# Tile 0 of a fused attention and mixture kernel: two up stages ahead of two down stages, a new row layout for the down weights, and earlier transposes of the probabilities

## Chip, cores and metric

One core of one Trainium2 chip. The metric is the device time of one launch in microseconds. Time before: 560.77 us, the median of 3 runs (560.01 to 561.48). The core's span in a profile is about 1.7 us shorter than the time of its run.

## The reference, cut to what matters

```python
# q, k, v: (8, 8, 576, 64); retention: scores * decay mask, no softmax
scores = scale * q @ k.T ; ret = scores * gamma ** (i - j) (i >= j) ; x = ret @ v   # -> (4608, 512)
p = domain_probs / (domain_probs.sum(-1) + 1e-9)                                    # (4608, 4)
for e in range(4):
    h = np.maximum(x @ w1[e], 0.0)          # "up":   512 -> 1024
    out += p[:, e:e+1] * (h @ w2[e])        # "down": 1024 -> 512
```

The 4608 tokens are handled in 9 tiles of 512. A batch has 576 tokens, so each ends with a remainder of 64 rows after four chunks of 128.

## The kernel before

An up stage of a tile is 8 steps (32 matmuls with 512 columns, one result tile `ph` a step), a down stage 4 steps (32 matmuls as well, result `po`). The program gives each engine its instructions in one fixed order. In the views, PE is TensorE (matmuls and transposes), PEld its weight loads, DVE is VectorE, ACT ScalarE, POOL GpSimd and SP SyncE; `wt_...` are weights. The plan `at(g, f)` puts attention work behind step g of a tile. Weights are cast from fp32 to bf16 on the way in, which goes through the POOL queue; q, k and v come through the SP queue.

```python
def load_rem(b, gate=None):                  # the 64-row remainder: raw_kr, raw_qr, raw_vr
    ...
        i = nc.sync.dma_start(out=state[b][n + "r"], in_=src[b, :, SM:S, :].rearrange("h p d -> p h d"))
        if gate is not None and n == "k":
            after(i, gate)                   # not before the DMA "gate" has landed
def load_w1(e, part=None): ...               # w1 of expert 0 in two halves of 512 columns, one tile
def load_w2(e): ...
    return nc.gpsimd.dma_start(out=wt2, in_=moe_w2[e].rearrange("(fc p) d -> p fc d", p=128))
...
next(tile0)                                  # first half of the first up matmuls
a0.O(*UNITS[3])
next(tile0)
w20 = load_w2(0)
late_constants()
for e in range(1, E):
    load_w1(e)
    load_w2(e)
load_rem(0, w20)
...
at(1, mixing_weights)                        # 4 transposes of the probabilities, then DVE
at(3, lambda: a0.cast_rem(nc.gpsimd))        # krb, qrb, vrb on POOL
at(20, a0.Trem)                              # PE transposes of qrb, krb
at(22, a0.Srem, a0.Srem_mask)
at(24, a0.Orem)                              # uses vrb
```

## Time and profile before

| | before |
|---|---|
| median of runs | 560.77 us |
| span of the profiled core | 559.2 us |
| PE busy | 545.6 us (98%) |
| PE stands for w2 of expert 0 | 1.74 us, 26.25 to 27.99 |
| PE stands for xT ahead of tile 1 | 0.78 us, before 86.76 |

The engine line and the clock line of the page of the kernel before (the clock has a digit for each fortieth of the span, 9 is 90% or more of full rate):

```profile
PE 545.6 (98%) x3469; PEld 262.5 (47%) x3530; DVE 165.7 (30%) x283; ACT 217.0 (39%) x371; POOL 109.8 (20%) x182
...
PEclk9999999999999999999999999999999999999999
```

PE is the limit, so time can be won only where PE stands, or does work that it need not do. The list of PE's waits up to 95 us, kernel before (in total, times, longest):

```profile
PE pt L437 <- POOL qm L427: 2.3, 3, 1.0
PE po L543 <- DMA wt_492<-in_moe_w_dram: 1.7, 1, 1.7
...
PE ph L514 <- DVE xT L329: 0.8, 1, 0.8
```

`wt_492` is w2 of expert 0. The timeline of the kernel before around it (start, length, engine, line, operation, then the idle time just before and what ended it):

```profile
17.50 0.61 PE L514 MATMUL ph<-xT,wt_269 128*128 128x256 bf16 x4
...
20.73 0.67 PE L206 MATMUL pp<-identf,probs_raw 36*128 36x36 f32 x4
...
27.96 0.72 SPq L115 DMA_DIRECT2D raw_kr<-in_k_dram  x1
...
27.99 6.86 PE L543 MATMUL po<-wt_492,hT 128*128 128x512 bf16 x31 [1.74 <-DMA wt_492<-in_moe_w_dram]
...
40.99 0.60 POOL L243 CAST qrb<-raw_qr 64x512 bf16<-64x512 f32 x1 [3.38 <-DMA raw_qr<-in_q_dram]
...
43.64 0.29 PE L261 MATMUL ptr<-ident,qrb 64*128 64x64 bf16 x4
```

Three things are to be read here. PE stands 1.74 us for w2. The loads of the remainder are issued at 27.96, the moment w2 of expert 0 has landed: that is the gate. And the remainder's transposes at 43.64 have two microseconds to spare after the cast of qrb at 40.99 to 41.59, so the remainder costs PE no waiting.

### The profile page before, as it was taken

To read this page: it belongs to the slowest core of one execution; us is meant where nothing else is said; L and a number is where in the kernel's file an instruction comes from. 1 tells how busy PE (TensorE), PEld (TensorE's weight loads), DVE (VectorE), ACT (ScalarE), POOL (GpSimd) and SP (SyncE) were. 2 spreads that over 40 slices of the span, in tenths; PEclk is the share of its full clock that TensorE was granted. 3 is DMA by queue.
4 is the path that set the end of the run, shared out by engine and by line. 5 is a ranking of instruction groups with operands and counts; after the bars stand their busy time and mean duration, and the time that the engine had idled before them with its cause. 6 is when DMAs were issued, how large, how long until landed. Compare 5 with 4: busy or idle time off the path is not lost.

```text
span 559.2 us, 8453 instructions
## 1 busy us (share of the span) xinstructions
PE 545.6 (98%) x3469; PEld 262.5 (47%) x3530; DVE 165.7 (30%) x283; ACT 217.0 (39%) x371; POOL 109.8 (20%) x182
## 2 busy tenths in 40 slices
PE   7899999999999999999999999999999999999997
PEld 4544455454445444444445444544444444444443
DVE  5402262253214520462035212542046202220222
ACT  6442344433353235323433334323532353335332
POOL 7611247026001520044002600250010000000000
PEclk9999999999999999999999999999999999999999
DMA  9999999591369025910594058803300100010001
GB/s 232 176 203 200 209 206 231 104 213 15 104 131 180 1 84 89 217 28 38 109 179 92 0 123 157 135 1 98 63 2 1 73 3 0 1 76 0 1 0 75
DMA packets 148277, 53.83 MB, mean 96 GB/s; under 512 B 130668, under 2 KB 142188, under 8 KB 148240
## 3 DMA queue, kind: packets, MB, share of 16 engines
q1 hardware_dynamic: 141296, 44.79, 39.2%
q0 software_dynamic: 6800, 8.39, 8.8%
q8 instruction: 27, 0.44, 0.4%
q10 hardware_dynamic: 144, 0.13, 0.1%
q14 instruction: 10, 0.08, 0.1%
HBM read 45.16 MB, written 9.44 MB: 98 GB/s over the span
## 4 chain that ended last, share of the span: by engine, by line
PE 94%; DMA 3%; POOL 1%; issue 1%; SPq 1%; DVE 0%
PE po L543 44%; PE ph L514 43%; DMA wt_492<-in_moe_w_dram 2%; PE o L351 1%; DMA raw_k<-in_k_dram 1%; PE o L365 1%; SPq L85 1%; POOL km L423 0%; PE sr L336 0%; PE orem L358 0%; PE ptc L297 0%; POOL wt_269 L125 0%; PE kvb L389 0%; PE kva L389 0%; PE oc L322 0%
## 5 line engine op out<-in xcount | busy, mean ns | idle before, releaser
L533 ACT ACTIVATE hT<-ph 128x512 bf16<-128x512 f32 x288 | 171.6, 597 | 274.6 <-PE ph L514 274.6
L543 PEld LDWEIGHTS <-hT 128*128 128x128 bf16 x1160 | 112.5, 98 | 134.6 <-DMA wt_492<-in_moe_w_dram 2.2
L549 DVE SCALAR_TENSOR_TENSOR acc<-po,probs,acc 128x512 f32<-128x512 f32 (+1 forms) x109 | 81.3, 746 | 234.6 <-PE po L543 226.8
L514 PE MATMUL ph<-xT,wt_504 128*128 128x512 bf16 x280 | 66.3, 379 | 0.5
L514 PE MATMUL ph<-xT,wt_269 128*128 128x512 bf16 (+1 forms) x303 | 64.2, 362 | 1.4 <-DVE xT L329 0.8
L543 PE MATMUL po<-wt_492,hT 128*128 128x512 bf16 x286 | 63.4, 379 | 1.8 <-DMA wt_492<-in_moe_w_dram 1.7
L543 PE MATMUL po<-wt_506,hT 128*128 128x512 bf16 x273 | 63.8, 379 | 0.8
L514 PE MATMUL ph<-xT,wt_500 128*128 128x512 bf16 x280 | 64.1, 379 | 0.5
L543 PE MATMUL po<-wt_510,hT 128*128 128x512 bf16 (+1 forms) x287 | 63.4, 373 | 0.5
L514 PE MATMUL ph<-xT,wt_508 128*128 128x512 bf16 x286 | 63.7, 379 | 0.2 <-issue 0.2
L543 PE MATMUL po<-wt_502,hT 128*128 128x512 bf16 x280 | 63.4, 379 | 0.4
L403 POOL CAST sbd<-ksum 64x256 bf16<-64x256 f32 x36 | 14.4, 399 | 221.2 <-DVE ksum L408 197.6
L514 PEld LDWEIGHTS <-wt_269 128*128 128x128 bf16 x312 | 30.0, 98 | 32.1 <-issue 0.9
L514 PEld LDWEIGHTS <-wt_508 128*128 128x128 bf16 x288 | 28.0, 98 | 33.3
L514 PEld LDWEIGHTS <-wt_500 128*128 128x128 bf16 x288 | 27.7, 98 | 33.4
L514 PEld LDWEIGHTS <-wt_504 128*128 128x128 bf16 x288 | 26.9, 98 | 30.3
L547 ACT ACTIVATE acc<-po,probs 128x512 f32<-128x512 f32 x36 | 24.7, 687 | 40.1 <-PE po L543 39.1
L235 POOL TENSOR_TENSOR km<-raw_k,gk 128x512 bf16<-128x512 f32 x28 | 29.2, 1043 | 13.9 <-DMA raw_k<-in_k_dram 9.5
L237 POOL CAST vm<-raw_v 128x512 bf16<-128x512 f32 x28 | 17.3, 616 | 41.8 <-PE o L351 34.9
L237 POOL CAST qm<-raw_q 128x512 bf16<-128x512 f32 x28 | 17.1, 611 | 7.4 <-DMA raw_q<-in_q_dram 7.2
L374 DVE TENSOR_TENSOR xT<-o,gq 128x512 bf16<-128x512 f32 x24 | 15.5, 686 | 7.6 <-PE o L365 7.6
L240 POOL TENSOR_TENSOR krb<-raw_kr,gk 64x512 bf16<-64x512 f32 x8 | 8.3, 1037 | 13.8 <-DMA raw_kr<-in_k_dram 13.2
(231 smaller groups left out, 238.7 us busy)
## 6 DMA issues: line engine op xcount, KB each, us to landing
out_dram<-acc SPq DMA_DIRECT2D x35, 256.0 KB, 2.0
raw_k<-in_k_dram SPq DMA_DIRECT2D x32, 256.0 KB, 5.0
raw_q<-in_q_dram SPq DMA_DIRECT2D x32, 256.0 KB, 5.1
raw_v<-in_v_dram SPq DMA_DIRECT2D x32, 256.0 KB, 5.2
wt_269<-in_moe_w_dram POOLq DMA_DIRECT2D x2, 512.0 KB, 5.6
wt_492<-in_moe_w_dram POOLq DMA_DIRECT2D x1, 1024.0 KB, 11.7
wt_500<-in_moe_w_dram POOLq DMA_DIRECT2D x1, 1024.0 KB, 14.5
wt_502<-in_moe_w_dram POOLq DMA_DIRECT2D x1, 1024.0 KB, 20.4
```

The lines of the kernel that those rows point to most:

```text
L85: nc.sync.dma_start(out=pairs_of(state[b][n, hf])[:, h], in_=src[b, h, 256 * hf:256 * hf + 256, :].rearrange("h (p j) d -> p h (j d)", j=2))
L235: eng.tensor_tensor(o, i, gk[:, c, :].unsqueeze(2).to_broadcast([128, H, D]), op=MULT)
L237: eng.tensor_copy(o, i)
L240: eng.tensor_tensor(self.r["k"], self.t["kr"], gk[:R, NCH, :].unsqueeze(2).to_broadcast([R, H, D]), op=MULT)
L351: nc.tensor.matmul(o[64 * j:64 * j + 64, c * C:(c + 1) * C], lhsT=self.m["v"][:, c, 2 * p + j, :], rhs=self.sT[p][:, j, c, :], start=(c == ...
L374: nc.vector.tensor_tensor(xT[:, p, b * S:b * S + SM], o, gq[:, p, 0:SM], op=MULT)
L403: eng.tensor_copy(sbd[r, n, :, r], src[r])
L514: nc.tensor.matmul(ph[:, ts], lhsT=w1_sb[e][:, dc, fc * 128:(fc + 1) * 128], rhs=xT[:, dc, n0 + ts.start:n0 + ts.stop], start=(dc == 0), s ...
L533: nc.scalar.activation(hT[:, fc, :], ph, Relu)
L543: nc.tensor.matmul(po, lhsT=hT[:, fc, ns * 128:(ns + 1) * 128], rhs=w2_sb[e][:, fc, d:d + w], start=(fc == 0), stop=(fc == NFC - 1))
L547: nc.scalar.activation(a, po, Copy, scale=pe)
L549: nc.vector.scalar_tensor_tensor(a, po, pe, a, op0=MULT, op1=ADD)
```

## The change

Intent: in tile 0 only, do up 0 and up 1 before down 0 and down 1, so that PE has work while w2 of expert 0 is still on its way (w1 of expert 1 is therefore loaded ahead of it, in two halves); load w2 with two neighbouring rows in each partition, so that one run in memory (fp32) is 4 KB long instead of 2 KB (the packet records count bf16 bytes); transpose the probabilities in the first wait for w1; take up tile 1 with two early pieces of 384 columns in place of three of 256.

With rows 2i and 2i+1 of a 256-row block in partition i, the hidden units of a block have to come out of the up stage even ones first, then odd ones. So the up stage reads its weight columns with a step of two.

```diff
-        return nc.gpsimd.dma_start(out=wt2, in_=moe_w2[e].rearrange("(fc p) d -> p fc d", p=128))
+        return nc.gpsimd.dma_start(out=wt2[:, :, :].rearrange("p (fo fi) d -> p fo (fi d)", fi=2),
+                                   in_=moe_w2[e].rearrange("(fo p fi) d -> p fo (fi d)", p=128, fi=2))
 ...
-                nc.tensor.matmul(ph[:, ts], lhsT=w1_sb[e][:, dc, fc * 128:(fc + 1) * 128],
+                w = w1_sb[e][:, dc, (fc // 2) * 256:(fc // 2 + 1) * 256].rearrange("p (f i) -> p f i", i=2)
+                nc.tensor.matmul(ph[:, ts], lhsT=w[:, :, fc % 2],
 ...
+        first = [ups(0), ups(1), downs(0), downs(1)] if nt == 0 else [ups(0), downs(0), ups(1), downs(1)]
 ...
-    tiles = [moe(nt, lead=3 if nt < 2 else 0) for nt in range(n_nt)]
+    tiles = [moe(0, lead=3, pause=True), moe(1, lead=2, cut=3 * NT // 4)] + [moe(nt) for nt in range(2, n_nt)]
 ...
+    transposed_probs()
     next(tile0)
     a0.O(*UNITS[3])
     next(tile0)
+    load_w1(1, 0)
+    load_w1(1, 1)
+    late_constants()
     w20 = load_w2(0)
-    late_constants()
-    for e in range(1, E):
+    load_w2(1)
+    for e in range(2, E):
         load_w1(e)
         load_w2(e)
     load_rem(0, w20)
 ...
-            for c, g in enumerate((40, 42, 44, 46)):
+            for c, g in enumerate((39, 41, 43, 45)):
```

Cut here: the constant `identf` is made earlier on POOL, and the chunk work of batch 1 at the end of tile 0 moves into the plan.

More of the change, by code (lines that the diff above doesn't have):

```diff
@@ L156 @@
     make_identity(nc, ident)
+    identf = const.tile([NTT, NTT], FP32)
+    nc.gpsimd.tensor_copy(identf, ident[:NTT, :NTT])
     tri2 = const.tile([128, 2, 128], BF16)
@@ L163 @@
     tri = const.tile([128, 128], BF16)
-    identf = const.tile([NTT, NTT], FP32)
     trir = const.tile([128, R], BF16)
@@ L176, in late_constants @@
                                 base=0, channel_multiplier=-1, pattern=[[1, 128]])
-        nc.gpsimd.tensor_copy(identf, ident[:NTT, :NTT])
     lgp = const.tile([128, NP], FP32)
@@ L201, with transposed_probs @@
     psm = const.tile([128, NTT], FP32)
-    def mixing_weights():
-        pp = ps_at.tile([128, E, NTT], FP32, tag="at", name="pp")
+    def transposed_probs():
+        pp = ps_mm.tile([128, E, NTT], FP32, tag="mm", name="pp")
         for e in range(E):
@@ L207, in mixing_weights @@
         nc.vector.tensor_copy(probs, pp)
+    def mixing_weights():
         nc.vector.tensor_reduce(psm, probs[:, :, :].rearrange("p e t -> p t e"),
@@ L506, in O, with moe @@
                                         gq[:, 2 * u:2 * u + 2, ts], op=MULT)
-    def moe(nt, lead=0):
+    def moe(nt, lead=0, cut=NT // 2, pause=False):
         n0 = nt * NT
@@ L513, in up, with ups @@
             for dc in range(NDC):
-                nc.tensor.matmul(ph[:, ts], lhsT=w1_sb[e][:, dc, fc * 128:(fc + 1) * 128],
+                w = w1_sb[e][:, dc, (fc // 2) * 256:(fc // 2 + 1) * 256].rearrange("p (f i) -> p f i", i=2)
+                nc.tensor.matmul(ph[:, ts], lhsT=w[:, :, fc % 2],
                                  rhs=xT[:, dc, n0 + ts.start:n0 + ts.stop], start=(dc == 0), stop=(dc == NDC - 1))
         acc = [apool.tile([128, Dm], FP32, tag="acc", name="acc") for _ in range(NSUB)]
-        for e in range(E):
-            hT = hpool.tile([128, NFC, NT], BF16, tag="hT")
-            for fc in range(NFC):
-                if e == 0 and fc < lead:
-                    if fc == 0:
-                        early = [ps_mm.tile([128, NT], FP32, tag="mm", name="ph") for _ in range(lead)]
-                        for x in range(lead):
-                            up(early[x], e, x, slice(0, NT // 2))
-                            if x != 1:
-                                yield
+        hTs = {}
+        def ups(e):
+            hT = hTs[e] = hpool.tile([128, NFC, NT], BF16, tag="hT", name="hT")
+            n = lead if e == 0 else 0
+            early = [ps_mm.tile([128, NT], FP32, tag="mm", name="ph") for _ in range(n)]
+            for x in range(n):
+                up(early[x], e, x, slice(0, cut))
+                if pause and x != 1:
+                    yield
+            for fc in range(NFC):
+                if fc < n:
                     ph = early[fc]
-                    up(ph, e, fc, slice(NT // 2, NT))
+                    up(ph, e, fc, slice(cut, NT))
                 else:
@@ L534, in moe, with downs @@
                 yield
+        def downs(e):
+            hT = hTs[e]
             for ns in range(NSUB):
@@ L553, in moe @@
                 yield
+        first = [ups(0), ups(1), downs(0), downs(1)] if nt == 0 else [ups(0), downs(0), ups(1), downs(1)]
+        for stage in first + [g for e in range(2, E) for g in (ups(e), downs(e))]:
+            yield from stage
     a0 = AttP(0)
     UNITS = [(hf, u) for hf in range(2) for u in range(2)]
-    tiles = [moe(nt, lead=3 if nt < 2 else 0) for nt in range(n_nt)]
+    tiles = [moe(0, lead=3, pause=True), moe(1, lead=2, cut=3 * NT // 4)] + [moe(nt) for nt in range(2, n_nt)]
     tile0 = tiles[0]
@@ L619 @@
             at(25, begin1)
-            for c, g in enumerate((40, 42, 44, 46)):
+            for c, g in enumerate((39, 41, 43, 45)):
                 at(g, lambda c=c: state["a1"].Tc(c))
-                if c < 3:
-                    at(g + 1, lambda c=c: state["a1"].Sc(c))
+                at(g + 1, lambda c=c: state["a1"].Sc(c))
                 if c > 0:
@@ L626 @@
                 at(g + 1, lambda c=c: state["a1"].kv(c))
+            at(47, lambda: state["a1"].Oc(3))
         elif nt + 1 < B:
@@ L654 @@
                 f()
-        if nt == 0:
-            state["a1"].Sc(3)
-            next(tiles[1])
-            next(tiles[1])
-            state["a1"].Oc(3)
 _INS = ['q', 'k', 'v', 'moe_domain_probs', 'moe_w1', 'moe_w2']
```

## The prediction

> **What bounds the kernel now.** TensorE: the page shows PE busy 545.6 of 559.2 us, and the chain of waits is 94% PE. A 128x512 matmul starts about every 0.216 us and hides its 98 ns weight load, so only PE idle time can be won. The list of waits and the timeline show: 1.74 us at 26.25-27.99, before tile 0's first down matmul (its w2 landed at 27.95); 0.75 us at 86.0 before tile 1 (waits for the last xT write); 0.6 us of PE time for the four fp32 transposes of probabilities at 20.7.
>
> **What the change should win.** Up 1 fills the 1.74 us. Its two halves should land near 24 and 28, needed at about 26 and 29.3; w2 of expert 0 lands where w1 of expert 1 did (32.97), needed at about 32.9. The transposes' new wait holds only some 0.3 us of slack: gain about 0.3. Tile 1 with two early columns of 384: 0.75 + 0.2. Sum about 3 us. Weight loads with a step of two elements should cost nothing: the Trainium skill ("SBUF — State Buffer", on cachelines) lets bf16 stride up to 8 elements free; this trace doesn't test it.
>
> **What it adds.** The loads of batch 0's 64-row remainder (raw_kr, raw_qr, raw_vr) are gated by w2 of expert 0. Before: gate 27.95, first packets at 31.9 (4 us behind the weight packets already queued), landings 36.57, 40.99, 45.77; the transposes of the remainder ran on PE at 43.6, with 2 us to spare. The packet records show both queues served one packet for one: beside 1,024-byte weight packets 308 of the 256-byte ones pass in 2 us, beside 2,048-byte ones only 180. The skill says the same ("DMA: Bandwidth & Descriptors", queues: round robin by packet). After the change the gate opens 5 us later (about 32.9), and w2 now also travels in 2,048-byte packets. Estimate: first packets at 36.9, each 128 KB (512 packets, 32 per engine, 179 ns a pair) takes 5.7 us: raw_kr lands about 43.8, raw_qr 49.7, cast on POOL 0.6, so the transposes can start at about 50.3. PE arrives there (still after plan step 20) at about 41.6 and, being in order, stands about 8.7 us. raw_vr (about 55.2) just meets the later use. Chunk loads end earlier and don't bind.
>
> A stop that long should also cool the clock: the skill ("TensorE: Matmul & The Clock Gate", Part 1) gives half rate after about 3.4 us idle until 3.4 us busy. This trace agrees: the first eight matmuls took 3.44 us, 0.43 each. Estimate: 2 us lost.
>
> **Sum on the critical path.** Remainder transposes start 6.8 us later than before; then +2.0 for the clock, -0.95 at tile 1: about +7.5 us, 560.8 -> 568. Range 561 to 571.5. Chances: faster by over 2% 0.01, within 2% 0.93, slower by over 2% 0.06.
>
> **What would show it.** List of waits: w2 wait under 0.5 us; a new PE wait of 6-9 us for the POOL cast of qrb (or its DMA) at about 41.6-50; matmuls of 0.43 us start to start just after it; transposes of probabilities before the first up matmul; tile 1 without its 0.75 us; weights ending near 60 us.
>
> **What would make it wrong.** If the remainder loads start sooner or get more than one packet in two, the stop shrinks and the time falls toward 557.5 (about 15%). If stepped weight loads are slow enough to show behind 512-column matmuls, 1,152 of them at 10 ns would add 11 us. If the clock stays up, 566.

## The result

| | before | after |
|---|---|---|
| median of runs | 560.93 us (560.01 to 561.71, 6 runs) | 567.08 us (566.53 to 567.91, 6 runs) |
| span of the profiled core | 559.2 us | 565.5 us |
| mean granted clock | 1.0 | 0.991 |
| remainder transposes start on PE | 43.64 us | 49.30 us |

The ratio is 1.011, with a 95% interval of 1.0097 to 1.0123: a little slower, inside the 2% that count as the same. A ratio here is the mean time of one kernel's runs over that of the other's of the same rounds, so not quite the ratio of the medians.

The engine line and the clock line of the page after, to be held against those of before:

```profile
PE 552.9 (98%) x3526; PEld 263.7 (47%) x3526; DVE 165.6 (29%) x283; ACT 216.8 (38%) x371; POOL 109.5 (19%) x183
...
PEclk9798999999999999999999999999999999999999
```

PE looks busier by 7 us, though it has no more to do. The second and fourth digits of the clock tell part of why: in those slices matmuls ran at half rate (about 0.43 us from one to the next instead of 0.22) and took longer, by about 4.3 us (an estimate: half of the 5.3 and 3.4 us of the stretches below). The rest is not to be read as work, as the trace before lacks matmul records: it has 3,469 for 3,530 weight loads, the trace after 3,526 for 3,526. PE's waits up to 95 us, kernel after:

```profile
PE ptr L264 <- POOL qrb L246: 2.7, 1, 2.7
PE ph L519 <- DMA wt_270<-in_moe_w_dram: 2.4, 1, 2.4
PE pt L440 <- POOL qm L430: 2.3, 3, 1.0
```

The waits for w2 and for xT are gone, as intended. Two new ones stand in their place. The timeline after, at both:

```profile
18.16 0.28 PE L519 MATMUL ph<-xT,wt_270 128*128 128x256 bf16 x1
...
20.83 0.82 PE L519 MATMUL ph<-xT,wt_270 128*128 128x256 bf16 x3 [2.38 <-DMA wt_270<-in_moe_w_dram]
...
32.17 0.73 SPq L115 DMA_DIRECT2D raw_kr<-in_k_dram  x1
...
48.65 0.60 POOL L246 CAST qrb<-raw_qr 64x512 bf16<-64x512 f32 x1 [4.72 <-DMA raw_qr<-in_q_dram]
...
49.30 0.29 PE L264 MATMUL ptr<-ident,qrb 64*128 64x64 bf16 x4 [2.68 <-POOL qrb L246]
```

At 18.16 one up matmul runs, and then the next three stand for `wt_270`, which is w1 of expert 0: the first half is there, but the second of the two loads is awaited. At 49.30 the remainder's transposes stand for qrb, whose load was issued after 32.17 instead of after 27.96. The stretches of the trace after (length, busy time of PE, PEld, DVE, ACT and POOL, then the granted clock as the third number from the end):

```profile
18.20:20.80 2.60, 0.25 (x2) 0.06 (x1) 0.41 (x2) 0.24 (x1) 2.41 (x7) 0.71 1.18 167
20.80:26.10 5.30, 5.27 (x41) 3.71 (x42) 2.02 (x6) 0.53 (x1) 2.81 (x4) 0.50 1.20 196
26.10:46.60 20.50, 20.50 (x98) 9.29 (x96) 0.00 (x0) 11.66 (x20) 1.04 (x1) 1.00 1.13 208
46.60:49.30 2.70, 0.02 (x1) 0.00 (x0) 0.75 (x1) 0.00 (x0) 0.60 (x1) 1.00 1.14 205
50.10:53.40 3.30, 3.30 (x9) 1.22 (x8) 0.48 (x2) 0.00 (x0) 0.00 (x0) 0.50 1.14 207
```

After each of the two stops PE worked at half rate. The clock records of the trace put these stretches at 19.32 to 26.14, so from within the first stop on, and at 50.04 to 53.45.

The chain of waits after tells which of the two stops the time hangs on:

```profile
19.15 13.01 DMA wt_507<-in_moe_w_dram
...
32.17 0.73 SPq L115
...
32.94 15.65 DMA raw_qr<-in_q_dram
...
48.65 0.61 POOL qrb L246
...
49.30 0.40 PE ptr L264 x8
```

It runs from w2 of expert 0 (`wt_507`) to the issue of the remainder's loads, through 15.65 us of raw_qr, to the cast and the transposes. The first stop is not on it.

From the trace's packet records, two counts that bear on the 15.65 us (packets begun in 2 us, all 16 engines; when the 1st, 513th, 1025th of the remainder's 256-byte packets began):

```
                       weight packets        remainder packets
before, 34 to 36 us    308 of 1,024 bytes    293
before, 40 to 42 us    179 of 2,048 bytes    173
after,  44 to 46 us    178 of 2,048 bytes    176
first, 513th, 1025th:  before 31.92, 35.50, 39.65    after 36.15, 42.00, 47.76
```

The two queues began about equally many packets, whatever their size. Beside 1,024-byte packets 128 KB of the remainder took 3.6 us; beside 2,048-byte packets it took 5.8 us. In both kernels the first packet began 4.0 us after the issue (27.96 to 31.92, 32.17 to 36.15). What these 4 us wait for is not shown.

The stepped weight reads cost nothing visible. An up stage of expert 1, 32 matmuls each, before (plain columns) and then after (step of two), from the two timelines:

```profile
34.91 7.07 PE L514 MATMUL ph<-xT,wt_500 128*128 128x512 bf16 x32
```

```profile
30.92 7.07 PE L519 MATMUL ph<-xT,wt_499 128*128 128x512 bf16 x32
```

Matmuls of this length could hide a slower weight load, so the weight loads themselves have to be looked at. They took 98 ns each both ways; the same weights, from the two pages:

```profile
L514 PEld LDWEIGHTS <-wt_500 128*128 128x128 bf16 x288 | 27.7, 98 | 33.4
```

```profile
L519 PEld LDWEIGHTS <-wt_499 128*128 128x128 bf16 x288 | 27.8, 98 | 33.3
```

### The profile page after: what moved, and what is told of

It reads as the page before. It is cut to its first block, busy times and chain, and to the rows that moved or that the text cites. A ratio compares the mean times of both kernels' runs of the same rounds, so it can differ in the third digit from the quotient of the medians.

```text
span 565.5 us, 8505 instructions
## 1 busy us (share of the span) xinstructions
PE 552.9 (98%) x3526; PEld 263.7 (47%) x3526; DVE 165.6 (29%) x283; ACT 216.8 (38%) x371; POOL 109.5 (19%) x183
## 4 chain that ended last, share of the span: by engine, by line
PE 91%; DMA 6%; POOL 2%; SPq 1%; issue 0%; DVE 0%
PE po L553 43%; PE ph L519 42%; DMA raw_qr<-in_q_dram 3%; DMA wt_507<-in_moe_w_dram 2%; PE o L354 1%; DMA raw_k<-in_k_dram 1%; PE o L368 1%; SPq L85 1%; POOL km L426 0%; PE orem L361 0%; PE sr L339 0%; PE ptc L300 0%; POOL wt_270 L125 0%; PE kvb L392 0%; PE kva L392 0%; POOL wt_499 L125 0%
## 5 line engine op out<-in xcount | busy, mean ns | idle before, releaser
L519 PE MATMUL ph<-xT,wt_270 128*128 128x512 bf16 (+3 forms) x308 | 66.5, 374 | 2.4 <-DMA wt_270<-in_moe_w_dram 2.4
L553 PE MATMUL po<-wt_509,hT 128*128 128x512 bf16 x288 | 65.7, 386 | 0.0
L553 PE MATMUL po<-wt_513,hT 128*128 128x512 bf16 x288 | 64.6, 379 | 0.0
L553 PE MATMUL po<-wt_507,hT 128*128 128x512 bf16 x288 | 63.6, 379 | 0.0
```

What stands on the lines that cost most here:

```text
L519: nc.tensor.matmul(ph[:, ts], lhsT=w[:, :, fc % 2], rhs=xT[:, dc, n0 + ts.start:n0 + ts.stop], start=(dc == 0), stop=(dc == NDC - 1))
L553: nc.tensor.matmul(po, lhsT=hT[:, fc, ns * 128:(ns + 1) * 128], rhs=w2_sb[e][:, fc, d:d + w], start=(fc == 0), stop=(fc == NFC - 1))
```

## The experiments

Theory G: the remainder's loads, opened later and served more slowly, set the time; the stop at the first up matmuls is hidden behind them. Rival F: the stop at the first up matmuls and the half rate after it, about 5 us together (2.4 us of standing, and half of the 5.3 us that PE worked at half rate, 2.6 us), are what the change lost.

Each ratio is to the kernel before in the same rounds, whose median was 560.93 us beside the kernel after, 561.60 beside e1 to e4, 560.96 beside e5 and e6, and 560.99 beside e7 and e8. The kernel after did not run in these rounds, so a difference of medians across rounds can be off by some 0.7 us, and the ratios are the better measure there.

### e1_split: no stop at the first up matmuls

The built program's list of instructions shows the stop's cause. In the kernel after, the second weight load of the first up matmuls waits for the second DMA of w1; in the kernel before, that wait comes 105 instructions later, at the fifth step. (Semaphores DMASW0 and DMASW1 belong to the two halves; the numbers are places among all PE instructions, from the recorded kernels built anew.)

```
before:  403 Ldweights wt1_269 [waits DMASW0]  ...  508 Ldweights wt1_269 [waits DMASW1]
after:   407 Ldweights wt1_270 [waits DMASW0]       409 Ldweights wt1_270 [waits DMASW1]
```

The edit gives each half a tile of its own. With it the second wait is back at the fifth step.

```diff
-            w1_sb.append(wpool.tile([128, NDC, F], BF16, tag=f"w1_{e}", name="wt1"))
+            w1_sb.append([])
         f = slice(0, F) if part is None else slice(part * F // 2, (part + 1) * F // 2)
+        wt1 = wpool.tile([128, NDC, f.stop - f.start], BF16, tag=f"w1_{e}_{part}", name="wt1")
+        w1_sb[e].append(wt1)
 ...
+                n = NFC // len(w1_sb[e])
-                w = w1_sb[e][:, dc, (fc // 2) * 256:(fc // 2 + 1) * 256].rearrange("p (f i) -> p f i", i=2)
+                w = w1_sb[e][fc // n][:, dc, (fc % n // 2) * 256:(fc % n // 2 + 1) * 256].rearrange("p (f i) -> p f i", i=2)
```

> The changed kernel with each half of w1 of experts 0 and 1 in a tile of its own, so that the second up matmul no longer waits for the second half. Theory G (the remainder loads, opened by w2 of expert 0, set the time): the first stop (2.4 us) and its half clock go, PE arrives at the remainder transposes at about 41.5 and waits there until about 49.3, 7 to 8 us; time unchanged or a little longer, 566 to 569 us. Rival F (the stop at the first up matmuls and the half clock after it, 5 us together, are what the change lost): about 562 us.

Measured: 567.52 us (566.99 to 568.64), ratio to before 1.0115 (1.0098 to 1.0132). The waits of PE after 18 us up to 95 us, e1, and below them the remainder's transposes in its timeline:

```profile
PE ptr L266 <- POOL qrb L248: 7.7, 1, 7.7
PE po L556 <- issue: 0.2, 1, 0.2
```

```profile
49.16 0.39 PE L266 MATMUL ptr<-ident,qrb 64*128 64x64 bf16 x4 [7.71 <-POOL qrb L248]
```

The stop at the first up matmuls is gone and the one at the remainder has grown from 2.7 to 7.7 us. The transposes start at 49.16 us, against 49.30. Five microseconds were won at 18 us and not one of them reached the end. Rival F falls.

### e2_gate: the remainder's loads opened earlier

```diff
-    load_w1(1, 0)
+    w11 = load_w1(1, 0)
 ...
-    w20 = load_w2(0)
+    load_w2(0)
-    load_rem(0, w20)
+    load_rem(0, w11)
```

> The changed kernel with the remainder loads opened by the first half of w1 of expert 1 (lands about 24) instead of w2 of expert 0 (lands 32.2). First remainder packets at about 28, raw_qr cast at about 41.3, PE arrives at 46.6. Theory G: the wait for qrb (2.7 us) and the second half-clock stretch (1.7 us lost) go, the first stop stays: 562 to 563.5 us. Rival F (the wait for qrb hardly matters): 566 us or more.

Measured: 561.87 us (561.48 to 562.10), ratio 1.0007 (0.9992 to 1.0022). The loads were issued at 24.68, qrb was cast at 41.10, and PE came to the transposes at 45.65 without a wait. By the ratios 5.8 us of the kernel after's time are gone (5.2 us by the medians). From the timeline of e2, and below it PE's waits after 18 us up to 120 us:

```profile
24.68 0.73 SPq L115 DMA_DIRECT2D raw_kr<-in_k_dram  x1
...
41.10 0.60 POOL L246 CAST qrb<-raw_qr 64x512 bf16<-64x512 f32 x1 [4.74 <-DMA raw_qr<-in_q_dram]
...
45.65 0.29 PE L264 MATMUL ptr<-ident,qrb 64*128 64x64 bf16 x4
```

```profile
PE ph L519 <- DMA wt<-in_moe_w_dram: 2.2, 1, 2.2
PE ph L519 <- issue: 0.2, 1, 0.2
```

One wait is left, the first stop, and now it is this one that the time pays for. Theory G holds. The time came out 0.1 us below the range; the half-rate stretch in this profile was 3.41 us long (22.31 to 25.72) instead of 6.83, and PE came to the transposes 0.95 us earlier than expected.

### e3_split_gate: both

The edits of e1 and e2 together.

> Both edits. Neither is enough alone; together theory G expects both stops and both half-clock stretches gone: 557 to 558.5 us, faster than both kernels; a remaining wait for qrb under 1 us (cast at about 41.3, PE there at about 41.5) and one for w2 of expert 0 under 0.7 us, as the remainder packets now share with it. Rival F: the same as e1, about 562.

Measured: 559.67 us (558.83 to 559.92), ratio 0.9966 (0.9951 to 0.9980). Faster than both kernels, but about 1.2 us over the expected range. The waits after 18 us up to 120 us, e3:

```profile
PE s L281 <- DMA qkT<-km: 1.3, 1, 1.3
PE ptr L266 <- POOL qrb L248: 0.7, 1, 0.7
PE ph L522 <- issue: 0.2, 1, 0.2
```

The 0.7 us was expected. The 1.3 us was not: PE, now early, meets the scores of batch 2 in tile 1 (at 105 us) before the DMA transposes that they read. A wait that was covered by a late PE came to light. No half rate is recorded between 5.6 and 558.6 us.

### e4_split_warm: what the half rate costs

e1 with work without use in the stop.

```diff
-            at(20, a0.Trem)
+            at(20, lambda: warm(32), a0.Trem)
```

> e1 with 32 idle 128x512 matmuls (6.9 us) ahead of the remainder transposes, in the time in which PE would stand. The transposes still start at about 49.3, but without a half-clock stretch after them: 1.5 to 2.5 us less than e1. If the half clock costs nothing there, the same as e1.

Measured: 566.17 us (566.05 to 566.75), 1.35 us under e1 by medians, and their runs don't overlap. The 32 matmuls lasted a little past the cast, so the transposes started at 49.88, 0.7 us later than in e1; the half rate behind them (in e1 until 52.23, so 3.1 us at half rate, 1.5 us lost) was not there. By the profiles this nets 0.8 us, and the spans differ by 0.7 (565.1 and 564.4). The range of 1.5 to 2.5 was too high, since it took the transposes to start on time. This profile also had a half-rate stretch at 11.26 to 18.09, among the small attention matmuls, which the others had not: the clock can fall there too, and from run to run. It did not noticeably lengthen the run: the other three runs of e4 had a mean clock of 1.0 and took 566.05 to 566.75 us, the profiled one 0.994 and 566.21.

### e5_plain: the order alone, with the old layout

The kernel after with both layout edits of the diff taken back.

> The changed kernel with the old layout of both weights (w2 rows 128 apart, w1 columns next to each other), order and all else as changed. The second up matmul does not wait for the second half, so no first stop. w2 travels in 1,024-byte packets again: it lands about 33, but the remainder packets get through faster beside it: qrb cast at about 47 to 48, PE there at about 41.5 to 42. Theory G: wait of 5 to 6 us and a half-clock stretch, 565 to 567 us. Rival F: about 562.

Measured: 565.34 us (564.79 to 566.01), ratio 1.0075 (1.0059 to 1.0090). The timeline of e5 at the remainder:

```profile
42.78 1.03 POOL L242 TENSOR_TENSOR krb<-raw_kr,gk 64x512 bf16<-64x512 f32 x1 [19.00 <-DMA raw_kr<-in_k_dram]
46.11 0.60 POOL L245 CAST qrb<-raw_qr 64x512 bf16<-64x512 f32 x1 [2.30 <-DMA raw_qr<-in_q_dram]
...
46.77 0.29 PE L263 MATMUL ptr<-ident,qrb 64*128 64x64 bf16 x4 [4.49 <-POOL qrb L245]
```

The gate opened at 32.18, as in the kernel after, and the cast of krb began at 42.78, as there (42.89). But qrb followed 3.3 us later instead of 5.8 (48.65 less 42.89), as most of raw_qr went beside 1,024-byte packets of w2. So the layout itself cost the remainder 2.5 us. The stop at the first up matmuls is absent here: it comes with the layout edits and not with the order. The wait, 4.5 us, was shorter than the 5 to 6 expected, as w2 landed at about 32.2 and not at 33.

### e6_layout_alone: the layout in the kernel before

The two layout edits of the diff in the kernel before, nothing else.

> The kernel before with the new layout of both weights alone. It brings the wait for the second half of w1 to the second up matmul: a stop of 2.4 to 3 us at about 17.7 to 20.6 and a half-clock stretch after it (2.6 us lost); the wait for w2 (1.74 us) goes. The remainder loads open at about 27, qrb cast at about 44, PE there at about 47, so no wait. 563.5 to 565 us.

Measured: 564.10 us (561.46 to 564.65), ratio 1.0036 (1.0007 to 1.0065). PE's waits, e6:

```profile
PE ph L516 <- DMA wt<-in_moe_w_dram: 2.6, 1, 2.6
...
PE ph L516 <- DVE xT L330: 0.8, 1, 0.8
```

The stop at the first up matmuls is there and the wait for w2 is gone; qrb was cast at 44.17 and its transposes ran at 47.25 unhindered. So the stop belongs to the layout edits. Of the two it is the stepped view of w1: the kernel before with that edit alone, built for this check and not run, has the wait at the second weight load (place 405), and with the w2 edit alone at its old place (508). One of four runs took 561.46. Only one run was profiled (half rate at 19.93 to 26.75), but the mean clock is 1.0 in that one, 0.993 to 0.997 in the others, whose spans were 2.5 to 3.2 us longer. So that run had next to no time at half rate; whether its stop was shorter too is not known.

### e7_best: the two waits of e3 given time

```diff
-            at(20, a0.Trem)
-            at(22, a0.Srem, a0.Srem_mask)
-            at(24, a0.Orem)
+            at(21, a0.Trem)
+            at(23, a0.Srem, a0.Srem_mask)
+            at(25, a0.Orem)
 ...
-            at(19 if nt == 1 else 17, lambda: state["A"].S([0, 1]))
+            at(21 if nt == 1 else 17, lambda: state["A"].S([0, 1]))
```

> e3 with its two remaining waits given time: the remainder of batch 0 one plan step later (21, 23, 25 instead of 20, 22, 24), and in tile 1 the scores of batch 2 at step 21 instead of 19. In e3 PE waited 0.7 us for qrb and 1.3 us for a DMA transpose there. If both waits were on the critical path, 2 us less than e3: 557.3 to 558.2 us, PE waits after 18 us all under 0.3 us. If they only hid others, 559 to 560 us.

Measured: 557.75 us (557.32 to 559.47), ratio 0.9948 (0.9934 to 0.9963). PE's waits of the whole run, e7, all before 18 us:

```profile
PE pt L442 <- POOL qm L432: 2.0, 3, 0.8
PE warm_out L143 <- DVE warm_in L138: 1.3, 1, 1.3
PE pt L442 <- ACT qm L430: 0.8, 1, 0.8
```

This is the version that the change was after, 3.2 us under the kernel before, and by the ratios 9.1 us under the kernel after. The time lies in the range expected if both waits were on the critical path. But against e3 it is 1.9 us by the medians and only 1.0 us by the ratios, and two of the six runs took 558.93 and 559.47, so that the two waits cost the full 2 us is not shown.

### e8_transposes_back: the transposes of the probabilities, at their old place

e7 with `transposed_probs()` called from `mixing_weights` again, in the PSUM pool of before.

> e7 with the four transposes of the probabilities back behind the second piece of up 0, as in the kernel before. By the traces the move freed about 0.6 us of PE time and cost 0.4 us ahead of the first up matmul, less what other waits there took in: 0.1 to 0.7 us longer than e7, at the edge of what five rounds tell apart.

Measured: 557.97 us (557.77 to 558.21), ratio to before 0.9944 (0.9932 to 0.9956). By medians 0.2 us longer than e7, by the ratios no longer at all. Inconclusive: what this part of the change is worth lies under what five rounds tell apart.

## Why the prediction was right

The time (567.08 against 568.0 forecast, range 561 to 571.5) and its main cause were right. Point by point:

- *"only PE idle time can be won"*, and the stepped weight loads free: right. 32 up matmuls took 7.07 us both ways, and a weight load 98 ns. The Trainium skill ("SBUF — State Buffer", the note on cachelines under "Door 1: The DMA port swizzle") lets bf16 stride up to 8 elements free, and this trace agrees at a step of two.
- *Up 1 fills the 1.74 us, and tile 1 loses its 0.75 us*: right. Neither wait is in the list after.
- *The remainder's loads start later and get through more slowly*: right, and shown by e2 (loads opened earlier: 5.8 us won by the ratios), e5 (smaller weight packets: 2.5 us earlier) and e1 (the first stop does not matter). Forecast for the gate about 32.9, first packet 36.9, transposes 50.3; measured 32.17, 36.15, 49.30. The forecast's 308 is the count of weight packets; of the 256-byte ones 293 passed. The Trainium skill ("DMA: Bandwidth & Descriptors", "Queues, rings and completion order") states round robin by packet, and the packet counts agree, 178 to 176 in two microseconds.
- *"PE wait of 6-9 us"* at the transposes, where PE *"arrives there (still after plan step 20) at about 41.6"*: wrong. PE arrived at 46.6 and waited 2.7 us. The step that failed is the arrival at 41.6: it counted up 0 and up 1 without a break, and so overlooked the stop of 2.4 us at the second up matmul and the 2.6 us lost at half rate after it. The built list of the changed kernel has the wait at the second weight load; the forecast did not take it up. The sum survived because a stop before 49.3 us is hidden by the wait at 49.3. e1 shows this: with the stop taken away PE arrives at 41.45 and waits 7.7 us (forecast about 8.7), and the time is the same. That is luck of the order, not foresight.
- *"Estimate: 2 us lost"* to the clock: the stretch behind the remainder's transposes lasted 3.41 us, so 1.7 us. Right in kind, 0.3 too large. But the ground given was a stop of 8.7 us and a rule of about 3.4 us idle, and half rate came after a stop of 2.7 us, which that ground does not cover: here, too, there was luck. In e1, where the stop was 7.7 us, the half rate began within it, at 45.40, and lasted until 52.23.
- *Sum*: transposes later by 5.66 us (49.30 less 43.64), clock 1.7, the wait ahead of tile 1 -0.78: 6.6 us, against 6.3 between the spans.

Why the second weight load waits for the other half is argued, not shown: the stepped view of w1 seems to be taken for a range that reaches into the other half when the program's waits are built. Shown is that the wait comes with the layout edits (e6 has it, e5 has not) and goes when the halves are separate tiles (e1). That the first weight load (columns from 0 of the tile's 4,096) does not wait and the second (from 1,024) does, while the other half begins at 512, fits the explanation but does not test it.

## What to carry to other kernels

When a load is moved back in a queue, look up what else is opened by its landing, and follow that chain to its first reader; here the gate moved by 4.2 us, to a reader with 2 us to spare. Two queues that shared the DMA engines got about equally many packets here, so larger packets for one slowed the other, though the last weights landed earlier (60.3 us instead of 64.6). And of two stops in a row only the later one may count, as here (e1): take away each alone and both together, and read the list of waits of the built program, before summing them.

## What the Trainium skill lacked or had wrong

- "DMA: Bandwidth & Descriptors" states round robin by packet, "≈9-17 descriptors typical" to a packet. It lacks the consequence that a queue of small packets loses share when the other queue's packets grow: 256-byte packets went at 293 in 2 us beside 1,024-byte ones and at 176 beside 2,048-byte ones, about as many as of the other queue each time. Whether a packet of the trace's records is a packet of the page is not shown.
- The same page ("Specifications") gives a first-byte latency of about 0.6 us for the SP path. With the weight queue busy the first packet began 4.0 us after the start of the issue (27.96 to 31.92; 32.17 to 36.15), against 1.1 us for the first load in the kernel before (0.81 to 1.94). No page gives a figure for that.
- "TensorE: Matmul & The Clock Gate" ("HAM oscillation") advises no gap over about 3.4 us. In the profiles, with stops of 2.2 us (e2), 2.4 us and 2.7 us (after) and 2.6 us (e6) half rate began within the stop or up to 1.6 us after it, for 3.41 or 6.83 us; with stops of 1.3 us (e3) and 1.74 us (before) it did not. But one run of e6 kept a mean clock of 1.0, and in e4 6.83 us of half rate began at 11.26 with no stop over 1.3 us before it, so these runs give no length that decides.
- No page says that a stepped view of a weight tile can make a matmul wait for a load of columns that it does not read (2.4 us here, none with separate tiles).
